# Feature attention with an MLP: the keys' maximum as a bias of the exponential, one-input maxima, and rounding moved to ScalarE

## The chip, the cores and the metric

The kernel runs on one core of a Trainium2 chip. The metric is the device time of one execution in microseconds (us). Five engines of the core work side by side, each through its own queue in order: TensorE (PE in the profile; its weight loads are listed as PEld), VectorE (DVE), ScalarE (ACT), GpSimd (POOL) and SyncE (SP), which here only issues the DMAs.

## The reference

Attention by features, then a two-layer MLP, all in float32. There are 8 batches of 8 heads, 576 tokens, head size 64, and 128 features.

```python
def phi(x):
    proj = np.einsum('bhsd,df->bhsf', x, w_phi)
    proj = proj - np.max(np.abs(proj), axis=-1, keepdims=True)
    return np.concatenate([np.exp(proj), np.exp(-proj)], axis=-1)
q_p, k_p = (phi(q), phi(k))
kv = np.einsum('bhsf,bhsd->bhfd', k_p, v)
z = np.sum(k_p, axis=2)
num = np.einsum('bhsf,bhfd->bhsd', q_p, kv)
den = np.einsum('bhsf,bhf->bhs', q_p, z)[..., None] + 1e-06
# x: (num / den) as 4608 tokens x 512
h = x @ w_in                     # 512 -> 2048
g = np.maximum(0.01 * h, h)
out = g @ w_out                  # 2048 -> 512
```

The maximum that is subtracted is one number per token and head.

## The kernel before

**Work.** Heads are taken two at a time: 4 pairs a batch, 32 pairs in all, each with a key phase (`k_phase`) and a query phase. A key phase projects the keys, takes the maxima, exponentiates and multiplies with the values into a small matrix per head; a query phase projects the queries, exponentiates, multiplies with that matrix, and divides. Its result goes into `ring`, a buffer of two batches. The MLP takes 18 blocks of 256 tokens out of `ring`, each in 16 steps over the hidden units (`layer1`, then, three steps later, `layer2`).

**Precision.** Matmuls read float32 words in a fast format (`F32R`). To keep float32 accuracy most operands are split into a rounded part (`...h`) and the rest (`...l`), and two or three matmuls are added. A split costs a cast and a subtraction. The first 8 pairs (`NK`, `NN`) use other forms of the phases; from pair 8 on the ones described here hold.

**Order.** The program is written as a stream of attention pieces (generators, one piece per `yield`) advanced between the MLP's steps. A scheduler orders each engine's instructions ahead of time, by priorities (attention goes ahead of the MLP) and by times that it assumes for each instruction. On the chip each engine then goes through its fixed order and waits where an operand or a buffer is not ready. Attention may run ahead until `ring` is full.

**Which engine does a step** is a table, `ENG` (line 35): a letter per turn, `a` for ScalarE, `v` for VectorE, `p` for GpSimd; what is not listed in a copy goes to ScalarE. `copy_` (lines 64 to 69) and `tt_` (lines 71 to 72) look it up, so their instructions all have the lines 67 (ACT), 69 (DVE) and 72 in the profile, and are told apart by the names of their tiles.

**Buffers.** `PBUFS` (line 34) gives PSUM buffers: 3 for `a` (projections and query products), 1 for `c` (the key-value product), 2 for `h` (layer 1) and 2 for `acc` (layer 2). SBUF tiles have the numbers in `BUFS` (line 33), else one.

**Key phase from pair 8 on** (lines 198 to 273). The keys are split on load (L67 and L202, tile `ks`) and the values too (tile `vh`). For each of three groups of tokens (two of 256 tokens, one of 64): PE projects (L232), ACT copies half of the sum out of PSUM and DVE adds the other half (L237, tile `pmk`: 128 tokens on partitions by head and feature). DVE takes the absolute maximum per token and head (L240, tile `m4`) and subtracts it from `pmk` (L245; two turns on DVE, one on POOL, the `ksub` entry of `ENG`). Then for each chunk of 128 tokens ACT takes two exponentials over both heads (L250 and L251, 256 columns each, with scale 1 and -1), the result is split (`kph` on ACT, `kpl` on POOL or DVE), and PE multiplies with the split values (L212). The product is copied out (`ek` from `c`), transposed (L282) and split into `kvh` and `kvl` (L294, L295).

**Query phase from pair 8 on** (`q_phase`, lines 361 to 430). The queries are split (L67 and L368, tile `qs`). PE projects with the features on partitions (L378, L379); DVE transposes in blocks of 32 x 32 out of PSUM (L380, tile `tq`), after which each partition holds, for 18 blocks of tokens, 32 of the 128 features. DVE takes the maximum in each block (L382, tile `m`: 128 partitions by 2 heads by 18). What is left is the maximum over the four groups of 32 partitions. Six small DVE steps do it (L384 to L389): copy the upper 64 partitions down, maximum, copy 32 down, maximum, copy back up to 64 and to 128. DVE subtracts (L396) and transposes back (L398, tile `mb`). For each half of the tokens ACT takes the two exponentials (L403, L404, tile `eq`), the result is rounded (tile `qh`, the `qh` entry of `ENG`, one cast of 128 x 576) and POOL subtracts (tile `ql`). PE multiplies with the key-value matrix (L415, L416, L418), ACT copies numerator and denominator out (L420, L421), DVE transposes and inverts the denominator (L424 to L427), and POOL multiplies in `ring`.

**MLP.** `split` rounds the block's tokens (`xh`, `xl`). `layer1` has three matmuls for each of four slices (L615, L616, L618); ACT evicts the hidden tile with the leaky ReLU (L622, tile `g`) and rounds it (`gh`), POOL subtracts (`gl`). `layer2` has three matmuls for each of two token tiles (L635 to L637); the block's result is copied out in turn by ACT and DVE (`o`) and stored.

Of the kernel before, what the change touches and what calls it, by code (L numbers as in the profile page):

```python
# [9 lines left out]
F32 = mybir.dt.float32  # L10
# [3 lines left out]
AF = mybir.ActivationFunctionType  # L14
ALU = mybir.AluOpType
AX = mybir.AxisListType

P = 128
B, H, S, D = 8, 8, 576, 64
NP = H // 2  # L20
F = 128
# [10 lines left out]
NK = 8  # L32
BUFS = {"kph": 2, "eq": 2, "m4": 2, "g": 2, "gh": 2, "gl": 2, "ql": 2}
PBUFS = {"a": 3, "c": 1, "h": 2, "acc": 2}
ENG = {"vh": "a", "kst": "v", "qh": "v", "o": "av", "kl": "pv", "kpl": "pppv", "ksub": "vvp", "l": "v"}
TINY = 2.0 ** -15
HUGE = 2.0 ** 16 * 1.875
PF = -10 ** 6
# [6 lines left out]
def attention_moe_kernel(ctx: ExitStack, tc: tile.TileContext, q, k, v, vt, w_phi, w_in, w_out, out):  # L45
    nc = tc.nc
# [4 lines left out]
    def ct(shape, dt, name):  # L51
        return cp.tile(shape, dt, tag=name, name=name)

    def st(shape, dt, tag):
        return sp.tile(shape, dt, tag=tag, name=tag, bufs=BUFS.get(tag, 1))
# [15 lines left out]
    def tt_(key, o, a, b, op):  # L71
        (nc.vector if pick(key) == "v" else nc.gpsimd).tensor_tensor(o, a, b, op=op)  # L72
# [23 lines left out]
    vh = ct([P, 10, 66], F32R, "vh")  # L96
# [44 lines left out]
    for j in range(2):  # L141
        r = slice(64 * j, 64 * j + 64)
        c = slice(F * j, F * j + F)
# [46 lines left out]
    def k_phase(i):  # L190
        nat = i < NK
        rk, rv = kraw.pop(i)
        ks = st([P, 2, S], F32R, "ks")
        kh, kl = ks[:, 0], ks[:, 1]
        if nat:
            copy_("kh", kh, rk)
            tt_("kl", kl, rk, kh.bitcast(F32), ALU.subtract)
        else:
            for j in range(2):
                o, n = slice(64 * j, 64 * j + 64), slice(64 - 64 * j, 128 - 64 * j)  # L200
                copy_("kh", ks[o, j], rk[o])
                nc.vector.tensor_tensor(ks[n, j], rk[o], ks[o, j].bitcast(F32), op=ALU.subtract)  # L202
            copy_("vh", vh[:, :, 0:64], rv[:, :, 0:64])
            for r, c in ((slice(0, P), slice(0, 8)), (slice(64, P), slice(8, 10))):
                tt_("vl", vl[r, c], rv[r, c, 0:64], vh[r, c, 0:64].bitcast(F32), ALU.subtract)
        if i + 1 < B * NP:
            load_k(i + 1)
        yield
        kvp = pt("c")

        def kv_mm(j, lt, rt, first=False, last=False):
            nc.tensor.matmul(kvp[0 : lt.shape[1], 256 * j : 256 * j + 256], lhsT=lt, rhs=rt,  # L212
                             start=first and j == 0, stop=last, skip_group_check=True)

        for g in range(3):
            w = 2 if g < 2 else 1
            r = slice(0, P) if g < 2 else slice(64, P)
            n = P if g < 2 else 64
            m4 = st([P, 4], F32, "m4")
            pmk = st([P, 4, F], F32, "pmk")  # L220
            if nat:
                pk = pt("a")
                for s in range(w):
                    t0 = (2 * g + s) * P if g < 2 else S - P
                    proj(pk, s, kh[:, t0 : t0 + P], kl[:, t0 : t0 + P])
                pkv = pk[r, 0 : 256 * w].rearrange("p (a f) -> p a f", f=F)
            else:
                for s in range(w):
                    t0 = (2 * g + s) * P if g < 2 else S - P
                    pk = pt("a")  # L230
                    for j in range(2):
                        nc.tensor.matmul(pk[:, 256 * j : 256 * j + 256], lhsT=ks[:, j, t0 : t0 + P],  # L232
                                         rhs=wq.rearrange("p a f -> p (a f)"), start=True, stop=True)
                    pk = pk[r].rearrange("p (j x f) -> p j x f", j=2, x=2)
                    x = pmk[r, 2 * s : 2 * s + 2]
                    copy_("pk", x, pk[:, :, 1])
                    nc.vector.tensor_tensor(x, pk[:, :, 0], x, op=ALU.add)  # L237
                    yield
                pkv = pmk[r, 0 : 2 * w]
            nc.vector.tensor_reduce(m4[r, 0 : 2 * w], pkv, axis=AX.X, op=ALU.max, apply_absolute_value=True)  # L240
            mb = m4[r, 0 : 2 * w].unsqueeze(2).broadcast_to([n, 2 * w, F])
            if nat:
                nc.vector.tensor_tensor(pmk[r, 0 : 2 * w], pkv, mb, op=ALU.subtract)
            else:
                tt_("ksub", pkv, pkv, mb, ALU.subtract)  # L245
            yield
            for s in range(w):
                c = 2 * g + s
                ek = st([P, 2, 256], F32, ("ek", "kph", "kpl")[c % 3] if nat else "ek")
                nc.scalar.activation(ek[r, :, 0:F], pmk[r, 2 * s : 2 * s + 2], AF.Exp)  # L250
                nc.scalar.activation(ek[r, :, F:256], pmk[r, 2 * s : 2 * s + 2], AF.Exp, scale=-1.0)  # L251
                if nat:
                    for j in range(2):
                        kv_mm(j, rv[r, 4 * j + c if c < 4 else 8 + j], ek[r, j], first=c == 0, last=c == 4)
                    yield
                    continue
                if c < 4:
                    kph = st([P, 2, 256], F32R, "kph")
                    kpl = st([P, 2, 256], F32R, "kpl")
                    copy_("kph", kph, ek)  # L260
                    tt_("kpl", kpl, ek, kph.bitcast(F32), ALU.subtract)
                    for j in range(2):
                        kv_mm(j, vh[:, 4 * j + c], kph[:, j], first=c == 0)
                        kv_mm(j, vl[:, 4 * j + c], kph[:, j])
                    for j in range(2):
                        kv_mm(j, vh[:, 4 * j + c], kpl[:, j])
                else:
                    kst = st([P, 2, 256], F32R, "kph")
                    copy_("kst", kst[r], ek[r])
                    nc.vector.tensor_tensor(kst[0:64], ek[r], kst[r].bitcast(F32), op=ALU.subtract)  # L270
                    for j in range(2):
                        kv_mm(j, vl[:, 8 + j], kst[:, j])
                        kv_mm(j, vh[:, 8 + j], kst[:, j], last=True)
                yield
        kvs = st([P, 2, 256], F32, "ek").rearrange("p a (b f) -> p a b f", b=2)[0:66]
        copy_("kvs", kvs, kvp[0:66].rearrange("p (a b f) -> p a b f", a=2, b=2))
        yield
        kvt = pt("c")
        kvtv = kvt[:, 0:264].rearrange("p (a b f) -> p a b f", a=2, b=2)
        for j in range(2):  # L280
            for t in range(2):
                nc.tensor.transpose(kvtv[:, j, t], kvs[:, j, t], ident[0:66, 0:66])  # L282
        if i < NN:
            kvh = st([P, 2, 2, P], F32, "kvh")
            nc.scalar.copy(kvh[:, :, :, 0:64], kvtv[:, :, :, 0:64])
            nc.scalar.copy(kvh[:, :, :, 64:P], kvtv[:, :, :, 64:65].broadcast_to([P, 2, 2, 64]))
            kvs_of[i] = kvh, None
        else:
            kvh = st([P, 2, 2, P], F32R, "kvh")
            kvl = st([P, 2, 2, P], F32R, "kvl")  # L290
            zb = kvtv[:, :, :, 64:65].broadcast_to([P, 2, 2, 64])
            copy_("kvh", kvh[:, :, :, 0:64], kvtv[:, :, :, 0:64])
            copy_("kvh", kvh[:, :, :, 64:P], zb)
            nc.vector.tensor_tensor(kvl[:, :, :, 0:64], kvtv[:, :, :, 0:64], kvh[:, :, :, 0:64].bitcast(F32), op=ALU.subtract)  # L294
            nc.vector.tensor_tensor(kvl[:, :, :, 64:P], zb, kvh[:, :, :, 64:P].bitcast(F32), op=ALU.subtract)  # L295
            kvs_of[i] = kvh, kvl
        yield
# [63 lines left out]
    def q_phase(i):  # L361
# [3 lines left out]
        for j in range(2):  # L365
            o, n = slice(64 * j, 64 * j + 64), slice(64 - 64 * j, 128 - 64 * j)
# [3 lines left out]
            load_q(i + 1)  # L370
        yield
        tq = st([P, 2, 2, U], F32, "tq")
        m = st([P, 2, 18], F32, "m")
        for j in range(2):
            for u in range(2):
                pq = pt("a")[:, 0:U]
# [3 lines left out]
                nc.vector.transpose(tq[:, j, u], pq)  # L380
                yield
            nc.vector.tensor_reduce(m[:, j], blocks(tq[:, j]), axis=AX.X, op=ALU.max, apply_absolute_value=True)  # L382
        ms = st([64, 2, 18], F32, "ms")
        nc.vector.tensor_copy(ms, m[64:128])  # L384
        nc.vector.tensor_tensor(m[0:64], m[0:64], ms, op=ALU.max)
        nc.vector.tensor_copy(ms[0:32], m[32:64])
        nc.vector.tensor_tensor(m[0:32], m[0:32], ms[0:32], op=ALU.max)
        nc.vector.tensor_copy(m[32:64], m[0:32])
        nc.vector.tensor_copy(m[64:128], m[0:64])  # L389
        yield  # L390
        kvh, kvl = kvs_of[i]
        dn = tq[:, 0]
# [1 line left out]
        for j in range(2):  # L394
            tj = blocks(tq[:, j])
            nc.vector.tensor_tensor(tj, tj, m[:, j].unsqueeze(2).broadcast_to([P, 18, 32]), op=ALU.subtract)  # L396
            mb = st([P, 2, U], F32, "mb")
# [3 lines left out]
            for u in range(2):  # L401
# [3 lines left out]
                qh = qhs[:, u]  # L405
# [5 lines left out]
            for u in range(2):  # L411
                qh, ql = es[u]
# [15 lines left out]
        x = ring[:, b % 2, hp]  # L428
# [293 lines left out]
```

## Time and profile before

| what | value |
|---|---|
| time, median of 3 runs | 1253.36 us (1252.39 to 1255.06) |
| time of the profiled execution | 1253.03 us |
| its span, first to last instruction | 1251.2 us |
| mean granted TensorE clock | 0.993 |
| PE busy | 1184.7 us, 7654 matmuls |
| DVE busy | 840.5 us, 1349 instructions |
| ACT busy | 804.3 us, 2048 instructions |
| POOL busy | 691.0 us, 724 instructions |

Busy time counts the stretches in which an engine has at least one instruction under way. An instruction that is held up after it has started counts as busy. A row of a group gives line, engine, operation, output and input tiles, shapes, the count, then busy us and mean ns of one, then the idle time just ahead of them with what ended most of it. A row of waits gives who waited for whom, the total in us, how many times, and the longest.

### The profile page before, as it was taken

The page shows a single profiled execution, that of the slowest core. Times are in us where ns is not written, and L with a number is a line of the kernel's source. Part 1 is how long each engine was busy: PE and PEld are TensorE (multiplying, and loading weights), DVE is VectorE, ACT ScalarE, POOL GpSimd, SP SyncE. Part 2 cuts the span into 40 slices and gives each one's busy share as a digit, 9 for nine tenths or more (in the row PEclk, how much of TensorE's full clock was granted, in tenths as well). Part 3 has the DMA queues.
Part 4 walks back from the last instruction along what each step waited for, and adds up shares of the span by engine and source line. Part 5 has one row for each costly group of instructions (what it writes and reads, how often), then busy time and mean ns, then how long its engine had stood idle before and what let it go on. Part 6 is the DMA issues. An engine that isn't in the chain of part 4 may idle for free. (4 is left out here: it accounts for less than half of the span.)

```text
span 1251.2 us, 21516 instructions
## 1 busy us (share of the span) xinstructions
PE 1184.7 (95%) x7654; PEld 1045.7 (84%) x7654; DVE 840.5 (67%) x1349; ACT 804.3 (64%) x2048; POOL 691.0 (55%) x724
## 2 busy tenths in 40 slices
PE   6889899999998999899999999999999999999998
PEld 5577688898887888788898888899997889999997
DVE  7999843478788877788888788854888887300000
ACT  6897865767667776666776667764776767433232
POOL 3233232457685776666676677764676867433232
PEclk9999999999998999999999999999999999999999
DMA  6544510211111101111111111020111110000000
GB/s 189 155 125 140 141 52 13 57 31 30 47 31 47 29 29 31 30 39 29 48 30 48 31 39 39 10 58 28 30 24 37 28 38 1 18 17 1 18 17 18
DMA packets 62779, 57.02 MB, mean 46 GB/s; under 512 B 45136, under 2 KB 46288, under 8 KB 62672
## 3 DMA queue, kind: packets, MB, share of 16 engines
q1 hardware_dynamic: 62672, 55.65, 15.8%
q8 instruction: 60, 0.98, 0.3%
q14 instruction: 47, 0.39, 0.1%
HBM read 46.20 MB, written 9.44 MB: 44 GB/s over the span
## 5 line engine op out<-in xcount | busy, mean ns | idle before, releaser
L72 POOL TENSOR_TENSOR gl<-g,gh 128x256 fp32r<-128x256 f32 x288 | 242.4, 846 | 275.1 <-ACT gh L67 214.7
L615 PE MATMUL h<-xh,w0h 128*128 128x256 f32 x1152 | 295.2, 284 | 6.7 <-ACT dn L567 2.2
L616 PE MATMUL h<-xh,w0l 128*128 128x256 f32 x1152 | 293.5, 282 | 1.3 <-DVE w0l L72 1.3
L615 PEld LDWEIGHTS h<-xh,w0h 128*128 128x128 f32 x1152 | 217.9, 189 | 18.7 <-ACT dn L567 3.0
L635 PE MATMUL acc<-w1h,gh 128*128 128x512 f32 x576 | 229.5, 399 | 2.9 <-DVE o L69 1.8
L636 PE MATMUL acc<-w1l,gh 128*128 128x512 f32 x576 | 228.0, 396 | 0.0
L616 PEld LDWEIGHTS h<-xh,w0l 128*128 128x128 f32 x1152 | 218.0, 189 | 11.5 <-DVE w0l L72 2.1
L637 PE MATMUL acc<-w1h,gl 128*128 128x512 f32 x576 | 218.3, 396 | 0.2 <-POOL gl L72 0.2
L618 PE MATMUL h<-xl,w0h 128*128 128x256 f32 x1152 | 201.7, 283 | 0.7 <-POOL xl L72 0.7
L622 ACT ACTIVATE g<-h 128x256 f32<-128x256 f32 x288 | 108.1, 383 | 133.0 <-PE h L618 93.1
L72 POOL TENSOR_TENSOR ql<-eq,qh 128x576 fp32r<-128x576 f32 x96 | 153.0, 1601 | 71.8 <-DVE qh L69 59.8
L618 PEld LDWEIGHTS h<-xl,w0h 128*128 128x128 f32 x1152 | 164.7, 189 | 3.1 <-POOL xl L72 2.0
L67 ACT CAST gh<-g 128x256 fp32r<-128x256 f32 x288 | 114.8, 404 | 70.4 <-PE acc L636 68.5
L72 POOL TENSOR_TENSOR kpl<-ek,kph 128x512 fp32r<-128x512 f32 x72 | 104.3, 1449 | 34.6 <-ACT kph L67 17.3
L635 PEld LDWEIGHTS acc<-w1h,gh 128*128 128x128 f32 x576 | 108.8, 189 | 16.7 <-DVE o L69 2.7
L637 PEld LDWEIGHTS acc<-w1h,gl 128*128 128x128 f32 x576 | 105.7, 188 | 19.1 <-POOL gl L72 1.3
L636 PEld LDWEIGHTS acc<-w1l,gh 128*128 128x128 f32 x576 | 109.1, 189 | 12.8
L69 DVE CAST qh<-eq 128x576 fp32r<-128x576 f32 x96 | 95.6, 1002 | 35.7 <-ACT eq L404 24.7
L250 ACT ACTIVATE ek<-pmk 128x256 f32<-128x256 f32 (+1 forms) x128 | 53.4, 417 | 64.8 <-POOL kpl L72 27.5
L69 DVE COPY o<-acc 128x512 f32<-128x512 f32 x17 | 11.5, 677 | 124.2 <-DMA out_dram<-o 124.0
L403 ACT ACTIVATE eq<-mb 128x288 f32<-128x288 f32 x96 | 42.2, 439 | 81.6 <-DVE mb L398 77.9
L72 POOL TENSOR_TENSOR ring<-ring,mb 128x576 f32<-128x576 f32 (+2 forms) x45 | 52.1, 1158 | 66.7 <-DVE mb L573 18.3
(227 smaller groups left out, 2505.6 us busy)
## 6 DMA issues: line engine op xcount, KB each, us to landing
out_dram<-o SPq DMA_DIRECT2D x35, 256.0 KB, 2.0
rk<-in_k_dram SPq DMA_DIRECT2D x30, 288.0 KB, 2.8
ring<-in_w_in_dram SPq DMA_DIRECT2D x16, 512.0 KB, 3.6
qh<-in_w_out_dram SPq DMA_DIRECT2D x16, 512.0 KB, 3.6
rq<-in_q_dram SPq DMA_DIRECT2D x28, 288.0 KB, 2.9
rv<-in_v_dram SPq DMA_DIRECT2D x30, 256.0 KB, 3.5
rv<-in_vt_dram SPq DMA_DIRECT2D x60, 32.0 KB, 2.9
f<-in_k_dram SPq DMA_DIRECT2D x2, 288.0 KB, 4.2
```

The lines of the kernel that those rows point to most:

```text
L67: nc.scalar.copy(o, i)
L69: (nc.vector if e == "v" else nc.gpsimd).tensor_copy(o, i)
L72: (nc.vector if pick(key) == "v" else nc.gpsimd).tensor_tensor(o, a, b, op=op)
L250: nc.scalar.activation(ek[r, :, 0:F], pmk[r, 2 * s : 2 * s + 2], AF.Exp)
L403: nc.scalar.activation(eq[:, 0], mb[:, u], AF.Exp)
L615: nc.tensor.matmul(ph, lhsT=weight(0, "h", ft)[:, d * P : d * P + P], rhs=xh[:, d], start=d == 0, stop=False)
L616: nc.tensor.matmul(ph, lhsT=weight(0, "l", ft)[:, d * P : d * P + P], rhs=xh[:, d], start=False, stop=False)
L618: nc.tensor.matmul(ph, lhsT=weight(0, "h", ft)[:, d * P : d * P + P], rhs=xl[:, d], start=False, stop=d == NP - 1)
L622: nc.scalar.activation(g, ph, AF.Prelu, alpha=0.01)
L635: nc.tensor.matmul(a, lhsT=gh[:, ts], rhs=weight(1, "h", ft), start=ft == 0, stop=False)
L636: nc.tensor.matmul(a, lhsT=gh[:, ts], rhs=weight(1, "l", ft), start=False, stop=False)
L637: nc.tensor.matmul(a, lhsT=gl[:, ts], rhs=weight(1, "h", ft), start=False, stop=ft == NFT - 1)
```

## The change

Three things change, all from pair 8 on, and one allocation.

- The `qh` entry of `ENG` goes from VectorE to ScalarE: the cast of the queries' exponentials to the fast format.
- In the key phase the subtraction of the maximum (the `ksub` step) goes. A second, small reduction on VectorE writes the negated maximum (`m4` now holds the maximum and its negative), and ScalarE's exponentials take it as their bias, one number per partition. As the bias differs between the two heads, the two exponentials of 256 columns of each chunk become four of 128.
- In the query phase the six small steps become six reductions with one input: four are over an axis of length one (a copy through the maximum) and two over a pair that lies side by side in the tile.
- The tile `m4` grows from 4 to 8 numbers a partition, `m` and `ms` to twice their size. For the first 8 pairs only the shape of `m4` changes.

```diff
-ENG = {"vh": "a", "kst": "v", "qh": "v", "o": "av", "kl": "pv", "kpl": "pppv", "ksub": "vvp", "l": "v"}
+ENG = {"vh": "a", "kst": "v", "qh": "a", "o": "av", "kl": "pv", "kpl": "pppv", "ksub": "vvp", "l": "v"}
...
-            m4 = st([P, 4], F32, "m4")
+            m4 = st([P, 2, 4], F32, "m4")
...
-            nc.vector.tensor_reduce(m4[r, 0 : 2 * w], pkv, axis=AX.X, op=ALU.max, apply_absolute_value=True)
-            mb = m4[r, 0 : 2 * w].unsqueeze(2).broadcast_to([n, 2 * w, F])
+            nc.vector.tensor_reduce(m4[r, 0, 0 : 2 * w], pkv, axis=AX.X, op=ALU.max, apply_absolute_value=True)
             if nat:
+                mb = m4[r, 0, 0 : 2 * w].unsqueeze(2).broadcast_to([n, 2 * w, F])
                 nc.vector.tensor_tensor(pmk[r, 0 : 2 * w], pkv, mb, op=ALU.subtract)
             else:
-                tt_("ksub", pkv, pkv, mb, ALU.subtract)
+                nc.vector.tensor_reduce(m4[r, 1, 0 : 2 * w], m4[r, 0, 0 : 2 * w].unsqueeze(2), axis=AX.X, op=ALU.max,
+                                        negate=True)
...
-                nc.scalar.activation(ek[r, :, 0:F], pmk[r, 2 * s : 2 * s + 2], AF.Exp)
-                nc.scalar.activation(ek[r, :, F:256], pmk[r, 2 * s : 2 * s + 2], AF.Exp, scale=-1.0)
+                if nat:
+                    nc.scalar.activation(ek[r, :, 0:F], pmk[r, 2 * s : 2 * s + 2], AF.Exp)
+                    nc.scalar.activation(ek[r, :, F:256], pmk[r, 2 * s : 2 * s + 2], AF.Exp, scale=-1.0)
+                else:
+                    for a in range(2 * s, 2 * s + 2):
+                        nc.scalar.activation(ek[r, a - 2 * s, 0:F], pmk[r, a], AF.Exp, bias=m4[r, 1, a : a + 1])
+                        nc.scalar.activation(ek[r, a - 2 * s, F:256], pmk[r, a], AF.Exp, bias=m4[r, 0, a : a + 1],
+                                             scale=-1.0)
...
-        m = st([P, 2, 18], F32, "m")
+        mm = st([P, 2, 2, 18], F32, "m")
+        m = mm[:, 0]
...
-        ms = st([64, 2, 18], F32, "ms")
-        nc.vector.tensor_copy(ms, m[64:128])
-        nc.vector.tensor_tensor(m[0:64], m[0:64], ms, op=ALU.max)
-        nc.vector.tensor_copy(ms[0:32], m[32:64])
-        nc.vector.tensor_tensor(m[0:32], m[0:32], ms[0:32], op=ALU.max)
-        nc.vector.tensor_copy(m[32:64], m[0:32])
-        nc.vector.tensor_copy(m[64:128], m[0:64])
+        def one(o, x):
+            nc.vector.tensor_reduce(o, x.unsqueeze(3), axis=AX.X, op=ALU.max)
+
+        ms = st([64, 2, 2, 18], F32, "ms")
+        one(mm[0:64, 1], m[64:128])
+        nc.vector.tensor_reduce(ms[0:64, 0], mm[0:64].rearrange("p s j c -> p j c s"), axis=AX.X, op=ALU.max)
+        one(ms[0:32, 1], ms[32:64, 0])
+        nc.vector.tensor_reduce(m[0:32], ms[0:32].rearrange("p s j c -> p j c s"), axis=AX.X, op=ALU.max)
+        one(m[32:64], m[0:32])
+        one(m[64:128], m[0:64])
```

## The prediction

> **What bounds the kernel now.** I first cut the span at the points where the attention work starts, pauses and ends, and read the busy time of each engine in each stretch (columns: stretch, its length, then PE, PEld, DVE, ACT and POOL busy, the granted clock, DMA share, GB/s).
>
> ```profile
> 250.00:813.00 563.00, 533.03 (x3520) 474.21 (x3518) 464.77 (x706) 390.42 (x1014) 379.23 (x367) 0.99 0.13 34
> 813.00:876.00 63.00, 63.00 (x422) 57.58 (x423) 31.00 (x52) 35.49 (x97) 35.59 (x41) 1.00 0.15 43
> 876.00:1063.00 187.00, 182.09 (x1235) 165.33 (x1234) 152.57 (x236) 133.50 (x351) 133.94 (x127) 1.00 0.10 26
> 1063.00:1251.20 188.20, 183.85 (x1164) 165.81 (x1162) 12.97 (x24) 62.30 (x164) 62.98 (x85) 1.00 0.04 15
> sum 1251.20, PE 1184.70 PEld 1045.73 DVE 840.51 ACT 804.33 POOL 690.97; mean PE 236.94 PEld 209.15 DVE 168.10 ACT 160.87 POOL 138.19
> ```
>
> The same view in 40 slices has one in which the granted clock is low long after the start:
>
> ```profile
> 375.40:406.60 31.20, 27.55 (x162) 23.30 (x161) 27.47 (x45) 22.56 (x57) 17.19 (x18) 0.89 0.17 47
> ```
>
> PE is the bound: it is idle for 66.5 us of 1251.2, and the change takes no matmul away. It can only move PE's idle time. The edits begin with pair 8 and leave the pairs before it alone, which are worked on before 250 us; the stretches from 813 to 876 and from 1063 us, where attention pauses and is over, have no idle but 4.4 us at the very end. What is left is 563.0 - 533.03 + 187.0 - 182.09 = 34.9 us in the 750 us in which attention and MLP share PE (27 us lie before them), and the slice with the clock at 0.89, which costs 0.11 x 31.2 = 3.4 us. So some 38 us is the most that there is to win.
>
> In those 750 us DVE is busy (464.77 + 152.57) / 750 = 82.3%, ACT 523.9 / 750 = 69.9%, POOL 513.2 / 750 = 68.4%. Who PE waits for there is said by its waits from 250 to 1063 us (columns: total us, times, longest):
>
> ```profile
> PE c L212 <- DVE kvl L295: 5.4, 7, 1.6
> PE c L212 <- POOL kpl L72: 3.8, 5, 1.9
> PE a L415 <- DVE qh L69: 3.6, 7, 0.7
> PE a L378 <- DVE tq L380: 3.1, 5, 1.1
> PE a L415 <- DVE pmk L237: 2.8, 7, 0.6
> PE a L415 <- ACT tq L421: 1.9, 3, 0.9
> PE a L418 <- POOL ql L72: 1.8, 3, 0.8
> PE acc L635 <- DVE o L69: 1.8, 2, 1.3
> ...
> PE c L212 <- DVE kpl L72: 0.2, 1, 0.2
> ```
>
> All 18 rows make 32.0 us: 19.1 behind DVE, 6.5 behind POOL, 6.4 behind ACT. The reader is to see that the waits are short and spread over many places, and that the fullest of the three helpers causes most of them.
>
> **The change part by part.** The rows that price what DVE and POOL lose (whole run; busy us, then mean ns):
>
> ```profile
> L69 DVE CAST qh<-eq 128x576 fp32r<-128x576 f32 x96 | 95.6, 1002 | 35.7 <-ACT eq L404 24.7 <-POOL ql L72 4.4 <-POOL gl L72 3.8
> L72 DVE TENSOR_TENSOR pmk<-pmk,m 128x512 f32<-128x512 f32 x48 | 46.6, 972 | 0.8
> L72 POOL TENSOR_TENSOR pmk<-pmk,m 64x256 f32<-64x256 f32 x24 | 17.0, 709 | 18.8 <-DVE m L240 12.4 <-PE a L379 2.5 <-PE a L232 2.4
> L386 DVE COPY ms<-m 32x36 f32<-32x36 f32 x24 | 12.1, 503 | 0.8
> L387 DVE TENSOR_TENSOR m<-m,ms 32x36 f32<-32x36 f32 x24 | 11.2, 466 | 0.8
> L385 DVE TENSOR_TENSOR m<-m,ms 64x36 f32<-64x36 f32 x24 | 11.1, 461 | 0.7
> L388 DVE COPY m<-m 32x36 f32<-32x36 f32 x24 | 9.3, 387 | 0.8
> L384 DVE COPY ms<-m 64x36 f32<-64x36 f32 x24 | 8.6, 359 | 0.6
> L389 DVE COPY m<-m 64x36 f32<-64x36 f32 x24 | 7.3, 304 | 0.8
> L240 DVE TENSOR_REDUCE m<-pmk 128x4 f32<-128x512 f32 x48 | 32.7, 681 | 1.3
> L240 DVE TENSOR_REDUCE m<-pmk 64x2 f32<-64x256 f32 x24 | 10.0, 417 | 0.8
> ```
>
> *Rounding of the queries' exponentials* (96 casts) leaves DVE: -95.6 us. *The subtraction of the keys' maximum* goes: -46.6 us on DVE, -17.0 on POOL. *The maximum over partition groups*: six small steps, 59.6 us in all, become six reductions. No row shows a reduction of 36 or 72 elements; the two reductions above lie on 153 ns + 1.03 ns an element, so four of 36 and two of 72 cost 4 x 190 + 2 x 227 = 1214 ns, 29.1 us over 24 pairs: -30.5. Bounds: nothing won if they wait as the small copies do (59.6), -33.9 if each costs what the copy of L386 took at its best (below, 0.17 to 0.18 us, so 25.7 in all). I take -30.5, since the reductions' row is the same operation. *The negated maximum* adds 72 reductions of 4 or 2 elements, 157 ns by the same line: +11.3. DVE in all: -95.6 - 46.6 - 30.5 + 11.3 = -161.4 us, POOL -17.0.
>
> Why the removed steps were so dear is seen in single instructions (start, duration):
>
> ```profile
> 646.63 0.17 DVE L386 COPY ms<-m 32x36 f32<-32x36 f32 x1
> ...
> 717.77 0.46 DVE L69 CAST qh<-eq 128x576 fp32r<-128x576 f32 x1 [1.46 <-ACT eq L404]
> 718.44 1.62 DVE L69 CAST qh<-eq 128x576 fp32r<-128x576 f32 x1 [0.21 <-ACT eq L404]
> ```
>
> The same cast takes 0.46 or 1.62 us, and a copy that takes 503 ns in the mean takes 0.17: much of the time is waiting inside the instruction. It is DVE's time all the same, and I count it. The Trainium skill (VectorE: DVE Perf Modes, the section on the trn2 errata) speaks against moving the cast: it gives an SBUF copy 58 cycles plus half a cycle an element in the double mode, 360 ns here, well under ACT's price below. The trace agrees only for casts like the first one; by the page DVE would gain 34.6 us of the cast, and the working below would end 2.7 us later, at 1244.9.
>
> What ACT takes on:
>
> ```profile
> L67 ACT CAST ks<-rk 128x576 fp32r<-128x576 f32 x6 | 4.0, 668 | 0.8 <-DMA rk<-in_k_dram 0.8
> L250 ACT ACTIVATE ek<-pmk 128x256 f32<-128x256 f32 x104 | 43.4, 417 | 46.3 <-POOL kpl L72 27.5 <-DVE pmk L72 18.4
> L251 ACT ACTIVATE ek<-pmk 128x256 f32<-128x256 f32 x104 | 42.1, 405 | 0.0
> L67 ACT CAST xh<-ring 128x256 fp32r<-128x256 f32 x48 | 17.1, 402 | 0.9 <-PE h L616 0.5
> L67 ACT CAST xh<-ring 128x128 fp32r<-128x128 f32 x16 | 3.5, 296 | 2.1 <-POOL ring L72 2.1
> ```
>
> And two exponentials in a row (start, duration):
>
> ```profile
> 610.75 0.42 ACT L250 ACTIVATE ek<-pmk 128x256 f32<-128x256 f32 x1
> 611.07 0.40 ACT L251 ACTIVATE ek<-pmk 128x256 f32<-128x256 f32 x1
> ```
>
> 96 casts of 128x576 at 668 ns: +64.1 us. The exponentials go from 240 of 256 columns to 480 of 128. Halving the columns saves 402 - 296 = 106 ns, so one costs 411 - 106 = 305 ns. Summed plainly that is 480 x 0.305 - 240 x 0.411 = +48 us; but one starts 0.09 us before the one ahead ends (610.75 to 611.07), so a slot is 0.211 against 0.317 us: +25 us, which I take, as they come four in a row. That the bias now comes from a tile is not shown in any row; bounds: no cost, or as dear as with 256 columns, 480 x 0.317 - 76 = +76 us. I take no cost, as a copy with no bias (402) and the exponential with its default one (405) differ by 3 ns.
>
> New shares over the 750 us: DVE (617.3 - 161.4) / 750 = 60.8%, POOL 66.2%, ACT (523.9 + 64.1 + 25) / 750 = 81.7%. The change adds no wait between engines, but moves one: the query cast overwrites what PE's products of the half before (L415, L416) and POOL's subtraction read, and it is now ACT that stands there. ACT's queue is in order: behind the cast stand the next exponentials, the eviction of the MLP's hidden tile (L622), its rounding and the copies out of PSUM, and PE waits for all of these. No DMA is moved and SP's queue stays as it is. The keys' exponentials no longer wait for a subtraction of 0.97 us, only for a reduction of 0.16.
>
> For the waits I take the queue rule that waiting goes with share/(1 - share), an estimate. DVE: 4.65 to 1.55, 19.1 us becomes 6.4. POOL: 2.16 to 1.96, 6.5 becomes 5.9. ACT: 2.32 to 4.47, 6.4 becomes 12.3: what is late next is ACT's eviction of the query products (L421), already its longest row. Sum 24.6 against 32.0: -7.4 us. The dip of the clock lies in a slice with 3.65 us idle, more than twice the mean of 34.9 / 24 = 1.45; with less idle I count it gone: -3.4. The profiled execution took 1253.03 us (span 1251.2), 0.3 under the median 1253.36: 1253.0 - 10.8 = 1242. All of DVE's waits and the dip gone with no more behind ACT: 1230.5. ACT's plain sum of 48 us (84.8%): its waits 15.4, total 1245; keeping the dip as well, 1249.
>
> **Rivals.** *A. The bias is dear.* At +76 us ACT is at 664 / 750 = 88.5%, its waits grow to 21.2, the sum to 33.5, the dip stays: 1254.5. For it: no row shows the form. The Trainium skill (ScalarE: Activation LUTs, What ACT_TABLE_LOAD costs) gives 93 ns more for each operand read from a tile, 480 x 93 ns = 44.6 us; by it the time would be 1253. No run here shows it.
>
> *B. ACT holds up the MLP: slower.* ACT evicts the hidden tile, which has two PSUM buffers (its group from 250 to 1063 us, and PE's wait for it):
>
> ```profile
> L622 ACT ACTIVATE g<-h 128x256 f32<-128x256 f32 x191 | 71.6, 382 | 52.8 <-POOL gl L72 30.7 <-PE h L618 18.9 <-PE a L232 1.5
> PE h L615 <- ACT g L622: 0.7, 1, 0.7
> ```
>
> With 191 evictions in 813 us a step lasts 4.26 us. One group of query exponentials with its cast is 1.36 us of ACT: two slots of 0.344 (288 columns: 0.317 and 32 columns at 106/128 ns) and 0.67. Once an eviction stands behind two such groups and the four exponentials of a key chunk, some 3.6 us, the next layer-1 group finds no buffer. If that comes once in each of the 48 halves of the 24 pairs, at 0.7 us as in the one wait seen, it adds 33.6 us: 1253.0 - 7.4 + 33.6 = 1279. For it: ACT would be as full as DVE is now, and unlike DVE it serves the MLP. Against it: only one such wait is seen today, with ACT at 69.9%.
>
> *C. The idle time is the order's.* If PE idles because its order fits the helpers badly wherever they stand, the waits only change names: 1253.
>
> **How the numbers follow.** Forecast 0.64 (of it 0.03 within 0.2%), A 0.12 (0.01 faster, 0.05 same, 0.06 slower), B 0.16 (slower), C 0.08 (0.02 faster, 0.05 same, 0.01 slower). That gives faster by over 0.2% (2.5 us, about what a measurement of this kernel can tell from no change) 0.64, same 0.13, slower 0.23. The range runs from 1229, just under the best case, to 1264, which takes in A and the milder half of B.
>
> **What would show it.** Right: DVE's busy time near 680 us, ACT's near 890, POOL's near 674; small reductions near 0.2 us each; PE's waits behind DVE well under 10 us; no clock under 1.00 after 250 us. Wrong: exponentials of 128 columns above 0.35 us (A), PE waiting in L615 for L622 many times (B), the same 32 us under other names (C), or an order of instructions that differs before pair 8.

## The result and the profile after

The changed kernel takes 1232.93 us (median of 4 runs, 1232.39 to 1233.62) against 1252.88 us before: a ratio of 0.9838, 95% interval 0.9821 to 0.9855. It is 20 us faster, where 11 were forecast. The profiled execution took 1233.62 us, its span is 1231.8.

The busy times of the page of the changed kernel:

```profile
PE 1176.5 (96%) x7654; PEld 1053.2 (85%) x7654; DVE 677.5 (55%) x1277; ACT 917.6 (74%) x2384; POOL 648.8 (53%) x700
```

VectorE lost 163.0 us, ScalarE gained 113.3, GpSimd lost 42.2. The same engines from 250 to 1063 us, first before, then after (columns as in the prediction):

```profile
250.00:1063.00 813.00, 778.12 (x5174) 697.12 (x5173) 648.34 (x992) 559.41 (x1460) 548.77 (x534) 1.00 0.12 33
```

```profile
250.00:1063.00 813.00, 792.80 (x5330) 725.77 (x5329) 486.45 (x921) 676.52 (x1805) 514.11 (x519) 0.98 0.12 34
```

PE's idle time in this stretch falls from 34.9 to 20.2 us, and 156 more matmuls are done in it; but the granted clock is lower. PE's waits in it, all 14 rows but the four smallest:

```profile
PE c L212 <- DVE ms L396: 3.6, 1, 3.6
PE a L426 <- ACT qh L67: 3.5, 4, 1.5
PE h L626 <- ACT g L633: 2.5, 3, 1.5
PE c L212 <- ACT kph L67: 1.8, 2, 1.3
PE a L426 <- ACT tq L432: 1.6, 2, 1.5
PE c L212 <- POOL kpl L72: 1.4, 3, 0.7
PE a L232 <- DVE ks L202: 1.1, 1, 1.1
PE c L212 <- DVE kpl L72: 1.0, 1, 1.0
PE a L386 <- DVE tq L388: 0.8, 1, 0.8
PE a L429 <- POOL ql L72: 0.8, 1, 0.8
...
```

By engine: VectorE 19.1 to 7.6 us, GpSimd 6.5 to 2.5, ScalarE 6.4 to 9.7, together 32.0 to 19.8. The steps that the prediction priced (groups of the changed kernel; L392 is the line of the four one-input copies, L396 and L398 the maxima over pairs, L245 the negated maximum):

```profile
L256 ACT ACTIVATE ek<-pmk,m 128x128 f32<-128x128 f32 x192 | 74.7, 397 | 7.4 <-POOL kpl L72 6.9
L257 ACT ACTIVATE ek<-pmk,m 128x128 f32<-128x128 f32 x192 | 74.2, 393 | 0.0
L67 ACT CAST qh<-eq 128x576 fp32r<-128x576 f32 x96 | 63.5, 671 | 0.5 <-PE a L427 0.3
L392 DVE TENSOR_REDUCE m<-m 64x36 f32<-64x36 f32 x48 | 8.8, 184 | 1.3
L396 DVE TENSOR_REDUCE ms<-m 64x36 f32<-64x72 f32 x24 | 5.3, 222 | 0.7
L398 DVE TENSOR_REDUCE m<-ms 32x36 f32<-32x72 f32 x24 | 5.3, 219 | 0.8
L245 DVE TENSOR_REDUCE m<-m 128x4 f32<-128x4 f32 x48 | 7.2, 149 | 1.2
```

The small reductions cost what the line through the two large ones gave. The exponentials do not: with a bias read from a tile 128 columns cost 0.39 us (that it is the bias is shown by a run below). Started in a row, each takes 0.30 us (start, duration, after):

```profile
388.97 0.39 ACT L257 ACTIVATE ek<-pmk,m 128x128 f32<-128x128 f32 x1
389.26 0.39 ACT L256 ACTIVATE ek<-pmk,m 128x128 f32<-128x128 f32 x1
389.55 0.39 ACT L257 ACTIVATE ek<-pmk,m 128x128 f32<-128x128 f32 x1
```

The largest difference against the change is one place, the stretch from 370 to 405 us, before and then after:

```profile
370.00:405.00 35.00, 29.71 (x176) 25.04 (x175) 31.57 (x52) 22.39 (x57) 22.16 (x24) 0.90 0.18 51
```

```profile
370.00:405.00 35.00, 24.14 (x113) 20.39 (x112) 25.41 (x54) 27.09 (x68) 14.95 (x13) 0.66 0.18 49
```

PE does 113 matmuls there instead of 176, at a mean clock of 0.66.

**A better measure of PE's loss.** PE's busy time hides waits. A matmul is listed at 0.28 us, but the next one starts 0.12 us later (before):

```profile
602.01 0.28 PE L616 MATMUL h<-xh,w0l 128*128 128x256 f32 x1
602.13 0.28 PE L615 MATMUL h<-xh,w0h 128*128 128x256 f32 x1
```

So PE can stand for up to 0.16 us without being listed as idle, at every wait. I therefore worked out from all starts in the trace how much later than its pace each matmul starts (the pace is the lower quartile before: 0.117 us for 256 columns, 0.131 for 288, 0.230 for 512). At this pace all 7654 matmuls take 1093.1 us in either kernel; the rest is loss, half clocks included: 147.6 us before, 128.5 after. By stretch (us of loss):

| kernel | time | 250-370 | 370-405 | 405-520 | 520-545 | 545-813 | 813-1063 | 1063-1100 |
|---|---|---|---|---|---|---|---|---|
| before | 1252.9 | 7.0 | 11.2 | 10.2 | 7.0 | 26.4 | 12.4 | 1.0 |
| after | 1232.9 | 2.1 | 22.0 | 1.8 | 10.3 | 6.5 | 5.8 | 5.3 |
| rounding only | 1228.1 | 4.9 | 20.2 | 2.3 | 1.5 | 13.8 | 7.2 | 0.5 |
| bias only | 1234.7 | 7.2 | 11.3 | 5.7 | 9.0 | 14.4 | 8.7 | 0.5 |
| maxima only | 1220.3 | 3.5 | 15.2 | 5.5 | 1.6 | 9.9 | 6.0 | 0.5 |
| bias and maxima | 1222.0 | 3.1 | 9.9 | 8.4 | 7.8 | 7.4 | 6.8 | 0.5 |
| after, rounding on VectorE to pair 15 | 1222.4 | 2.8 | 10.6 | 7.4 | 7.4 | 3.0 | 6.3 | 5.3 |
| after, rounding in turns | 1233.4 | 2.0 | 23.1 | 2.6 | 10.0 | 8.6 | 6.6 | 0.5 |
| after, no bias | 1203.1 | 4.1 | 14.9 | 1.3 | 0.2 | 3.4 | 3.1 | 0.5 |
| after, three waits lifted | 1227.6 | 2.1 | 4.9 | 4.0 | 0.3 | 11.7 | 23.9 | 0.6 |
| before and an idle reduction | 1237.1 | 7.0 | 10.7 | 6.8 | 2.2 | 18.6 | 13.0 | 0.5 |
| maxima, rounding from pair 16 | 1211.2 | 3.5 | 15.2 | 5.5 | 1.5 | 4.3 | 2.8 | 0.5 |

Outside the two stretches at 370 to 405 and 520 to 545 us, which I call the stops, the loss from 250 to 1063 us falls from 56.0 us before to 16.2 after. In the stops it rises from 18.2 to 32.3. A loss is that of the profiled execution, a time the median of all; they belong together to within 2 us but for "after, no bias", whose profiled execution took 1207.7 us.

### The profile page after: what moved, and what is told of

Its sections match the earlier page's. It is cut to its first block, busy times and chain, and to the rows that moved or that the text cites. A ratio compares the mean times of both kernels' runs of the same rounds, so it can differ in the third digit from the quotient of the medians.

```text
span 1231.8 us, 21734 instructions
## 1 busy us (share of the span) xinstructions
PE 1176.5 (96%) x7654; PEld 1053.2 (85%) x7654; DVE 677.5 (55%) x1277; ACT 917.6 (74%) x2384; POOL 648.8 (53%) x700
## 3 DMA queue, kind: packets, MB, share of 16 engines
q1 hardware_dynamic: 62672, 55.65, 15.9%
## 4 chain that ended last, share of the span: by engine, by line
PE 51%; DVE 2%; ACT 2%; issue 1%; POOL 0%; ACTq 0%; DVEq 0%; POOLq 0%
PE h L626 7%; PE h L629 7%; PE h L627 7%; PE acc L646 7%; PE acc L647 7%; PE acc L648 7%; PE c L212 4%; PE a L429 1%; PE a L427 1%; PE a L426 1%; PE a L232 1%; PE a L386 1%; PE a L387 1%; DVE qs L375 0%; DVE tq L388 0%
## 5 line engine op out<-in xcount | busy, mean ns | idle before, releaser
L72 POOL TENSOR_TENSOR gl<-g,gh 128x256 fp32r<-128x256 f32 x288 | 231.3, 808 | 288.9 <-ACT gh L67 235.3
L648 PE MATMUL acc<-w1h,gl 128*128 128x512 f32 x576 | 214.5, 396 | 0.4 <-POOL gl L72 0.3
L72 POOL TENSOR_TENSOR ql<-eq,qh 128x576 fp32r<-128x576 f32 x96 | 139.8, 1465 | 34.1 <-ACT qh L67 26.8
L72 POOL TENSOR_TENSOR kpl<-ek,kph 128x512 fp32r<-128x512 f32 x72 | 100.2, 1391 | 47.9 <-ACT kph L67 35.6
L202 DVE TENSOR_TENSOR ks<-rk,ks 64x576 fp32r<-64x576 f32 x48 | 50.1, 1043 | 96.6 <-ACT ks L67 95.8
L257 ACT ACTIVATE ek<-pmk,m 128x128 f32<-128x128 f32 (+1 forms) x240 | 90.7, 392 | 10.9 <-DVE m L240 8.7
L256 ACT ACTIVATE ek<-pmk,m 128x128 f32<-128x128 f32 (+1 forms) x240 | 91.0, 394 | 8.1 <-POOL kpl L72 6.9
L237 DVE TENSOR_TENSOR pmk<-a,pmk 128x256 f32<-128x256 f32 (+1 forms) x120 | 48.0, 421 | 76.8 <-ACT pmk L67 75.1
```

The costliest lines, as they stand in the source:

```text
L256: nc.scalar.activation(ek[r, a - 2 * s, 0:F], pmk[r, a], AF.Exp, bias=m4[r, 1, a : a + 1])
L257: nc.scalar.activation(ek[r, a - 2 * s, F:256], pmk[r, a], AF.Exp, bias=m4[r, 0, a : a + 1], scale=-1.0)
L648: nc.tensor.matmul(a, lhsT=gl[:, ts], rhs=weight(1, "h", ft), start=False, stop=ft == NFT - 1)
```

## The experiments

Two questions: which part makes the gain, and what the stops are. The load theory: PE's scattered waits fall as VectorE is emptier. Its rival: the change only makes the scheduler find another order. The result of each part alone came first.

**The parts.** The rounding alone:

```diff
-ENG = {... "qh": "v", ...}
+ENG = {... "qh": "a", ...}
```

> The kernel before with the rounding of the queries' exponentials on ScalarE and nothing else. Load theory (PE's short waits fall because VectorE is emptier): VectorE near 745 us, ScalarE near 868 us, and the larger part of the 20 us, about 1239 us. Rival (the gain comes from another order of the instructions, not from the load): any time from 1233 to 1260, with no relation to what VectorE has left to do.

Measured: 1228.12 us, ratio 0.9797 (0.9783 to 0.9812). VectorE 740.3, ScalarE 856.2 us: 100.2 us less for 96 casts, a little more than the theory has, and 51.9 more, 12 less than it has. The gain of 26 us is larger than that of the whole change.

The bias alone (the key phase of the diff above, `qh` on VectorE, the six old steps):

> The kernel before with the keys' maximum as a bias and nothing else. Load theory: VectorE 47 us less and 11 us more for the negated maxima, ScalarE up by some 60 us as an exponential with a bias tile takes 0.39 us (0.30 us from start to start); little left of the gain, 1248 to 1253 us. Rival (order): anything from 1233 to 1260 us.

Measured: 1234.69 us, ratio 0.9847 (0.9831 to 0.9864). VectorE 796.5, ScalarE 866.7 us. The loads are about right (VectorE loses 44 us instead of 36, ScalarE gains 62), the time is not: 19 us faster where 0 to 5 were expected.

The maxima alone (the query phase of the diff above and nothing else):

> The kernel before with the six one-input maxima and nothing else. Load theory: VectorE about 32 us less, ScalarE as before, about 1247 us. Rival (order): as far from before as the other two parts, in either direction.

Measured: 1220.27 us, ratio 0.9731 (0.9717 to 0.9746). VectorE loses 21.8 us, less than the 32 expected, and ScalarE nothing, and the kernel is 34 us faster, more than with any other single part. From the first of the six steps to the end of the last it takes 3.8 us in the mean before and 2.2 here, by their starts and ends in the two traces.

Bias and maxima, the rounding back on VectorE:

```diff
-ENG = {... "qh": "a", ...}
+ENG = {... "qh": "v", ...}
```

> The changed kernel with the rounding of the queries' exponentials back on VectorE. Load theory: about 1244 us, the sum of the gains of the bias and of the maxima within 4 us. Rival (order): no such sum.

Measured: 1222.00 us, ratio 0.9751 (0.9737 to 0.9766). The two gains, 19 and 34 us, don't add up: together 32. With the rounding on top it is 20, so the rounding, which wins 26 us alone, costs 11 there. Each part wins more alone than the load theory allows, and all three together win less than two. In its simple form the theory falls.

One part of it does better than the time. The loss outside the stops, added up from the table, mostly goes with VectorE's busy time: 56.0 us at 840.5 us busy (before), 36.0 at 796.5 (bias only), 28.2 at 740.3 (rounding only), 16.2 at 677.5 (after); the maxima alone lie well below that row (24.9 at 818.7). As each of these kernels also has another order, this is not a proof.

**Is it the order?** A reduction whose result nobody reads was added to each key phase from pair 8 on, in three kernels. It costs VectorE 3.5 us in all (group of the kernel before with it):

```profile
L247 DVE TENSOR_REDUCE ty<-m 128x4 f32<-128x4 f32 x24 | 3.5, 147 | 0.0
```

```diff
                 tt_("ksub", pkv, pkv, mb, ALU.subtract)
+                if g == 0:
+                    nc.vector.tensor_reduce(st([P, 4], F32, "ty"), m4.unsqueeze(2), axis=AX.X, op=ALU.max)
```

In the kernel before:

> The kernel before with one more reduction of 128x4 on VectorE in each key phase from pair 8 on, whose result nobody reads (24 x 0.15 = 3.6 us of VectorE). It changes no work that matters, but shifts the order that the scheduler makes. Theory that the parts of the change act by what they take away: 1252 to 1258 us. Rival (the order of before is an unlucky one, and each edit wins by making another): 1245 us or less, or a clear step the other way.

Measured: 1237.07 us, ratio 0.9866 (0.9851 to 0.9881). Work that nobody needs makes the kernel before 16 us faster. Its page:

```profile
PE 1179.1 (95%) x7654; PEld 1044.2 (85%) x7654; DVE 835.4 (68%) x1373; ACT 804.3 (65%) x2048; POOL 691.7 (56%) x724
```

ScalarE and GpSimd are as busy as before to within 1 us, VectorE is busy for 5 us less in spite of the 3.5 us added. What differs is the order: PE's first 2300 or so matmuls are the same, and 5547 of the 7654 can be matched in the same sequence. What is left to make this gain is the order of the instructions (the new tile may also move others in memory, which no run separates).

With the maxima:

> The kernel before with the six one-input maxima, and the same idle reduction. Theory that the maxima act by what they take away: as the maxima alone, 1218 to 1225 us. Rival (order): away from it by 8 us or more.

Measured: 1218.98 us, ratio 0.9721 (0.9706 to 0.9736), 1.3 us from the maxima without it. The order changed less here: 7177 of PE's 7654 matmuls can be matched with the maxima alone.

In the changed kernel (the same two lines, on the first half of `m4`):

> The changed kernel with the same idle reduction. Theory that the order matters little: 1230 to 1237 us. Rival (order): away from it by 8 us or more, as the three parts that win 19 to 33 us each alone and 20 together would suggest.

Measured: 1233.80 us, ratio 0.9841 (0.9822 to 0.9860), 0.9 us from the changed kernel. But the addition made no other order here: VectorE, ScalarE and GpSimd run the same sequence as in the changed kernel, and PE's differs in two matmuls.

So the kernel before takes 1253 us in one order and 1237 in another. That the other two kernels stay where they are doesn't make it the odd one: one of them had the same order again, the other one much like it. What another order would do to the changed kernel no run shows. Against the second order of before the change as a whole wins 4 us, and the maxima 17 to 18. That the maxima help is seen in both pairs, and again beside the bias (1234.7 to 1222.0 us); how large the whole change is apart from the order is not: 4 or 20 us, by the two orders of before and the one of after.

**What the stops are.** At 370 to 405 us PE has nearly nothing of the MLP to do. From 371.0 to 399.3 us it starts no matmul of the MLP at all, before the change from 377.9 to 392.1. Between 376 and 403 us the MLP has only this (groups of the changed kernel; before, it has 48 matmuls of layer 1 and 16 of layer 2 in these 27 us):

```profile
L629 PE MATMUL h<-xl,w0h 128*128 128x256 f32 x8 | 2.3, 415 | 0.0
...
L626 PE MATMUL h<-xh,w0h 128*128 128x256 f32 x2 | 0.8, 415 | 0.0
L627 PE MATMUL h<-xh,w0l 128*128 128x256 f32 x2 | 0.8, 415 | 0.0
```

The reason can be counted in the code. Attention writes `ring`, which holds two batches of 576 tokens, and the MLP takes blocks of 256. Batch 2 needs the place of batch 0, which is free when block 2 is split; block 4 needs batch 2. So four pairs have the time of two blocks, and four pairs take about 140 us (their key phases start 35 us apart). For batches 3, 6 and 7 it is two blocks as well, for 4 and 5 three. To test it, three blocks were made to take the tokens of the newer batch from the older one:

```diff
-                x = ring[:, c // S, d, c % S : c % S + n]
+                late = i in (4, 6, 15) and c // S == (i * T // S + 1) % 2
+                x = ring[:, 1 - c // S, d, 0:n] if late else ring[:, c // S, d, c % S : c % S + n]
```

> The changed kernel in which MLP blocks 4, 6 and 15 take the tokens that belong to the newer batch from the older one (so the output of these tokens is another), which lets the MLP run one block further before it needs the newer batch. Theory that the stops at 370 to 405, 520 to 545 and 1088 us are the MLP waiting for a batch: they shrink to a few us, no granted clock of 0.5 there, about 1205 us. Rival (the stops come from the attention's own work on PE): they stay, 1230 us or more.

Measured: 1227.55 us, ratio 0.9790 (0.9766 to 0.9815). The three stops go (22.0 to 4.9, 10.3 to 0.3, 5.3 to 0.6 us), but a new one comes, at the end of batch 5 (its last product is at 823 us; 815 to 840 us of this kernel):

```profile
815.00:840.00 25.00, 16.93 (x77) 13.68 (x76) 19.00 (x39) 18.39 (x50) 11.15 (x11) 0.66 0.21 59
```

So the stops are the MLP waiting for a batch, as stated, and the expected 1205 us were wrong: the attention is hardly earlier (its last matmul at 1083 us instead of 1087), and the wait moves on. It seems that in the changed kernel the attention's own pace has become a bound: its pairs follow each other without a pause, and 140 us of MLP remain behind them, while before the attention started no matmul from 840 to 863 us, and ended at 1078 us with 168 us left.

What paces them? With the rounding of the first eight such pairs on VectorE (`copy_` counts the casts, four a pair):

```diff
-ENG = {... "qh": "a", ...}
+ENG = {... "qh": "v" * 32 + "a" * 64, ...}
```

> The changed kernel with the rounding of the queries' exponentials on VectorE for pairs 8 to 15 and on ScalarE from pair 16. Theory: at 370 to 405 us and 520 to 545 us the MLP has no block left until a batch of attention is done, and there ScalarE's chain paces the attention; with the cast off ScalarE these two stops shrink to what they were before the change (18 us of lost PE time instead of 32), the rest stays: about 1220 us. Rival (the stops come from the longer chain of any engine, or VectorE is as slow): 1233 us or more.

Measured: 1222.40 us, ratio 0.9752 (0.9732 to 0.9772). The stops fall from 32.3 to 18.0 us, as expected, and the stretch without the MLP at the first is again 14 us long. The attention's last matmul ends at 1075 us instead of 1087, and the kernel is 10.5 us faster than the changed one, which fits the attention's pace as the bound. The first stop (the row to set beside the two above):

```profile
370.00:405.00 35.00, 29.89 (x181) 25.47 (x180) 26.27 (x48) 27.06 (x73) 23.22 (x22) 0.90 0.14 42
```

With the casts in turns on the two engines (`"qh": "av"`):

> The changed kernel with the rounding of the queries' exponentials on ScalarE and VectorE in turns. Theory that ScalarE paces the attention and that VectorE's load makes PE's short waits: ScalarE near 886 us, VectorE near 715 us, stops shorter, short waits somewhat up: about 1227 us. Rival (each cast on VectorE brings its waits back): 1240 us or more.

Measured: 1233.39 us, ratio 0.9832 (0.9807 to 0.9856). ScalarE 891.2 and VectorE 722.8 us are as expected, the stops are not shorter (33.1 us). Half of the casts on VectorE help nothing, all of them halve the first stop. Why half is not enough stays open. Over the table the first stop goes with the cast (20 to 23 us where all or half of these casts are on ScalarE, 10 to 15 where none is, 14.9 without the bias operand, and 4.9 with the wait lifted), the second with the bias (7.4 to 10.3 us with it, 0.2 to 2.2 without, but 7.0 before, and 0.3 with the wait lifted).

Without the bias operand:

```diff
-                        nc.scalar.activation(ek[r, a - 2 * s, 0:F], pmk[r, a], AF.Exp, bias=m4[r, 1, a : a + 1])
-                        nc.scalar.activation(ek[r, a - 2 * s, F:256], pmk[r, a], AF.Exp, bias=m4[r, 0, a : a + 1],
-                                             scale=-1.0)
+                        nc.scalar.activation(ek[r, a - 2 * s, 0:F], pmk[r, a], AF.Exp)
+                        nc.scalar.activation(ek[r, a - 2 * s, F:256], pmk[r, a], AF.Exp, scale=-1.0)
```

> The changed kernel with no bias in the keys' exponentials (they are taken of the projections as they are, so the keys' maximum is left out of the result); the maxima are still taken and negated. Theory that the bias tile has its price: an exponential of 128 columns takes 0.30 us instead of 0.39, ScalarE's busy time falls by about 40 us, the stops shorten, 1222 to 1230 us. Rival (128 columns cost 0.39 us with or without a bias): duration and time as the changed kernel, 1233 us.

Measured: 1203.13 us, ratio 0.9603 (0.9576 to 0.9629); ScalarE 876.0 us. The same groups as above:

```profile
L256 ACT ACTIVATE ek<-pmk 128x128 f32<-128x128 f32 x192 | 58.9, 307 | 24.9 <-POOL kpl L72 20.6 <-DVE pmk L237 3.8
L257 ACT ACTIVATE ek<-pmk 128x128 f32<-128x128 f32 x192 | 57.6, 300 | 0.0
```

The operand costs 90 to 93 ns each time, 41.6 us of ScalarE, and taking it away makes the kernel 30 us faster. This kernel also frees the exponentials from the wait for the maximum; which of the two the 30 us belong to wasn't separated.

Last, the parts that the runs speak for: the maxima, no bias, and the rounding on ScalarE from pair 16 on.

> The kernel before with the six one-input maxima, and the rounding of the queries' exponentials on ScalarE from pair 16 on; no bias. Theory that the bias costs more on ScalarE (0.39 us for each of 480) than it spares VectorE, and that the first eight pairs should keep ScalarE free: ScalarE near 845 us, VectorE near 755 us, about 1212 us, the shortest that gives the reference's output. Rival (order): anything from 1210 to 1235 us.

Measured: 1211.23 us, ratio 0.9658 (0.9643 to 0.9673), the fastest that computes the whole reference: 22 us faster than the change, 42 than before.

```profile
PE 1165.0 (96%) x7654; PEld 1046.5 (86%) x7654; DVE 754.8 (62%) x1285; ACT 840.0 (69%) x2112; POOL 681.0 (56%) x724
```

VectorE and ScalarE are as busy as expected to within 5 us; they stand nearer to each other than in the changed kernel (85 us apart instead of 240), though not as near as before (36). Outside the stops it loses 16.1 us from 250 to 1063 us, as little as the changed kernel, in the stops 16.7 instead of 32.3. Up to 545 us its losses are those of the maxima alone; the 9 us between these two kernels arise behind that, where the casts have left VectorE (7.1 us of loss from 545 to 1063 us instead of 15.9).

## Why the prediction was right or wrong

**Right in direction and within its range; the size is 20 us, not 11, and the agreement is luck in good part.** The forecast had two terms, -7.4 us for PE's scattered waits and -3.4 for the clock. By PE's starts the loss outside the stops fell by 39.8 us, and the stops and the stretch near 1092 us, where the clock is, took back 18.4. Two errors of opposite sign cancel in large part; and an edit that does nothing wins 16 us on the same kernel. Point by point:

- *VectorE.* -161.4 us forecast, -163.0 measured. The six reductions cost 0.18 to 0.22 us (forecast 0.19 and 0.23). For the cast it was right to go by the row: by the estimate from the Trainium skill's copy cycles (VectorE: DVE Perf Modes, the section on the trn2 errata, where the page itself says that they under-predict a single operation) 34.6 us would have come free; the rounding alone freed 100.2. Even the cast of 0.46 us that the prediction calls in agreement is longer than the 0.36 of that estimate.
- *GpSimd.* -17.0 forecast, -42.2 measured. The steps that stayed became shorter too, such as the subtraction of the rounded exponentials, from 1601 to 1465 ns:

```profile
L72 POOL TENSOR_TENSOR ql<-eq,qh 128x576 fp32r<-128x576 f32 x96 | 139.8, 1465 | 34.1 <-ACT qh L67 26.8
```

- *ScalarE.* +89 forecast, +113.3 measured. By the runs of the single parts the casts came cheaper (51.9 us instead of 64.1, as they too start before the one ahead ends), the exponentials dearer (62.4 instead of 25). This is the term of the sum that was wrong: the bias was taken at no cost and has 41.6 us of it, most of what rival A set for it (76 - 25 = 51). The Trainium skill (ScalarE: Activation LUTs, What ACT_TABLE_LOAD costs) has 93 ns for it; the runs show 90 to 93. The sign set for rival A, exponentials above 0.35 us, came; its 1254.5 us did not follow.
- *PE's waits.* 24.6 us forecast for the listed ones, 19.8 measured: VectorE 6.4 and 7.6, ScalarE 12.3 and 9.7, GpSimd 5.9 and 2.5. The rule of share/(1 - share) gave about the right sizes for VectorE and ScalarE, but the idle reduction shows that such agreement proves little: with the loads as they were, the listed waits of the kernel before fall from 32.0 to 22.6 us.
- *The ceiling.* The step that failed first: "some 38 us is the most that there is to win" was read from PE's idle time. By its starts PE lost 74 us from 250 to 1063 us, of which 34.9 are listed as idle and 3.4 are the clock; most of the rest hides behind matmuls that are listed until after the next one could have started. The gain outside the stops, 40 us, is larger than the ceiling.
- *The clock.* The step that failed next: "with less idle I count it gone: -3.4". The dip became worse. By the trace's record of the clock it is at half for 34.1 us from 250 us on, in the two stops and near 1092 us, against 6.8 before, all from 386 us on (the last few us of the span left out): at most 17 us lost instead of 3.4. The dip was taken for an effect of scattered waits. It lies in a stop, where the MLP has run out of tokens, and the change lengthened the first stop by its casts: with them on VectorE its loss is 10.6 us again instead of 22.0.
- *Rival B* (the MLP's eviction behind ScalarE's queue): three waits, 2.5 us, not 48. ScalarE's load does harm, but through the attention's pace.
- *Rival C* (the idle time is the order's) was priced at no change and given 0.08. It was the wrong way to think of it. An order that fits badly can be replaced by a better one through any edit, and for the kernel before there is such a better order: 16 of the 20 us are also won by an edit that does nothing. How much of the change's own gain came in this way is not shown.

What is settled: the maxima win in all three pairs of kernels that differ by them (13, 18 and 34 us), the bias operand costs ScalarE 41.6 us, the stops are waits for a batch, and the rounding of pairs 8 to 15 on ScalarE lengthens the first. What stays open: the share of the order in the 20 us, and why the single parts exceed the loads that they remove.

## What to carry to other kernels

Where a scheduler fixes the order ahead of time, change nothing of substance once or twice before believing a per cent: here a dead instruction was worth 16 us in one kernel, and 1 us in two others. Look whether the order did change: in one of these two it did not, so the small difference says nothing of how much the order matters there. Read PE's loss from the starts of its matmuls, not from its busy time, and look for places where one of two streams has nothing left to do, since there the slower stream's chain counts at its full length. A helper engine that is relieved at another's expense should be relieved only where the other isn't what such a place waits for.

## What the runs showed of the hardware

- A `[128, 1]` bias read from a tile makes an exponential of 128 columns cost 393 to 397 ns instead of 300 to 307; the default bias costs next to nothing (a cast of 128 columns takes 296 ns). Two exponentials in a row overlap by 0.09 to 0.10 us in the median either way.
- Reductions with one input kept their time beside a busy GpSimd (178 to 184 ns for 36 elements), where copies of the same 36 elements took 304 to 503 ns in the mean and 0.17 us at their best. Sorted by whether GpSimd had an instruction under way in the copy's first 0.15 us (before), the copies' four groups take 541 to 741 ns in the mean with it and 171 to 177 without; the reductions (after) take 181 and 182.
- The clock was halved where PE was far from idle. In the kernel before it went to half at 386.4 us: in the 3.4 us ahead of that PE started 9 matmuls, is listed as busy for 0.55 of the time, and has no wait over 0.8 us. In the changed kernel it went to half at 375.7 us, at a wait of 3.6 us, but also at 389.3, with no wait over 1.6 us in the 3.4 us ahead; from 370 to 405 us PE is listed as busy for 24.14 of 35 us, at a mean clock of 0.66.
